# Attention followed by a squared-ReLU feed-forward: the matrix engine takes the two products of the feed-forward in runs of four steps instead of two

## The chip, the cores and the metric

The kernel runs on one core of a Trainium2 chip. The metric is the device time of one execution in microseconds (us); the median of several executions is compared. The engines of a core work side by side, each through its own instructions in order: PE (TensorE, matrix products), ACT (ScalarE), DVE (VectorE), POOL (GpSimd) and SP (SyncE, which here only issues DMAs). In the profile PE is split into the matmuls (PE) and the loads of their stationary operand (PEld).

## The reference

```python
# attention: 4 batches, 8 heads, 768 rows, 64 columns
k_sum = k.reshape(B, H, nb, 32, D).max(axis=3)          # one key per block of 32
v_sum = v.reshape(B, H, nb, 32, D).mean(axis=3)
scores_l = scale * q @ k^T                               # only |i - j| < 16 counts
scores_s = scale * q @ k_sum^T + log(32)
a = softmax(concatenate([scores_l masked, scores_s]))
x = a @ concatenate([v, v_sum])                          # 3072 tokens x 512
# feed-forward
h = x @ w_in                                             # 3072 x 2048
g = s * relu(h) ** 2 + b
out = g @ w_out                                          # 3072 x 512
```

## The kernel before, in words

The 3072 tokens are taken in 12 **chunks** `c` of 256 tokens (three to a batch), and the 2048 hidden columns in 16 slices `f` of 128. One (chunk, slice) is a **step** `i = 16 c + f`; there are 192. A step has:

- `hidden(c, f)` on PE (line 364): the first product, `ph`. From the second chunk on each operand is split into a high and a low part (`wh`, `wl`, `xh`, `xl`), so that a slice is 12 matmuls of 256 columns: four `wl_in` with `xh`, four `wh` with `xl`, four `wh` with `xh`.
- `activate(c, f)`: ACT takes the ReLU out of PSUM (line 371) and squares it (372), POOL makes `g = s r + b` (382), DVE rounds it to `gh` (384) and takes the rest `gl` (386).
- `project(c, f)` on PE (line 401): the second product, for each half of the chunk's tokens `gl` with `wh`, `gh` with `wl_out` and `gh` with `wh`: six matmuls of 512 columns a step, summed over all 16 slices in two banks `po`. At the chunk's end `evict` copies `po` out (409) and SP sends it (412).

While the feed-forward of one chunk runs, the attention of the next is done between its steps, in four units `p` of two heads: `scores` into `ps` (PE, 266), `masked` (DVE, 285), `exps` (ACT, 298), `normalize` (DVE, 305 to 308), `transposes` of the probabilities into `pt` (PE, 314), `turned`, their copy `pT` (ACT, 321), `values` into `pav` (PE, 334, which reads `pT` and the windows `vw`), and `attended`, which copies `pav` to `xh` and `xl` (347, 349). POOL's `fill_k` and `fill_v` (239, 244) put the block keys and values beside the windows.

The order is written out by hand. `at(step, order, fn, ...)` puts a call into a table, and the table is played by step and, within a step, by these classes:

```python
LOAD, SPLIT, ATT, WEIGHTS, HID, PE_ATT, CHAIN, PROJ, EVICT = range(9)
```

Each engine gets its instructions in that order. An attention unit stands at `base` (two steps before the middle or the end of the chunk ahead of its own; units come in twos) plus a lag for each of its parts, from the lists `lags`. Two lines set the order of the products:

```python
at(i if c == 0 else i - i % 2, HID, hidden, c, f)
at(i + LAG if i + LAG < NF else (i + LAG) | 1, PROJ, project, c, f)
```

So from the second chunk on PE does the first product of two steps, then the second product of the two steps before them, and so on. The results of the first product lie in `ph` tiles of one step each; there are two of them, each in a PSUM bank of its own (banks 2 and 3). `gh` and `gl` have four buffers each. All eight banks are in use.

Of the kernel before, what the change touches and what calls it, by code (L numbers as in the profile page):

```python
# [10 lines left out]
F32 = mybir.dt.float32  # L11
F32R = mybir.dt.float32r
# [6 lines left out]
P = 128  # L19
# [7 lines left out]
KR = WIN + NB  # L27
NSUB = 4
T = NSUB * SUB
# [5 lines left out]
NF = DFF // P  # L35
NEG = -8.0e9
LAG = 2


def win_start(st):  # L40
    return min(max(SUB * st - WINDOW, 0), S - WIN)
# [3 lines left out]
def windowed_attention_then_relu2_ffn(ctx, tc, qk, vwin, kt, vt, kq, vrow, wp, sb, out):  # L45


    nc = tc.nc
# [5 lines left out]
    p2 = ctx.enter_context(tc.tile_pool(name="p2", bufs=2))  # L54
    p3 = ctx.enter_context(tc.tile_pool(name="p3", bufs=3))
    ps_po = ctx.enter_context(tc.tile_pool(name="ps_po", bufs=2, space=bass.MemoryType.PSUM))
    ps_h = ctx.enter_context(tc.tile_pool(name="ps_h", bufs=2, space=bass.MemoryType.PSUM))
# [31 lines left out]
    def at(step, order, fn, *args):  # L89
        plan[step].append((order, len(plan[step]), fn, args))  # L90
# [5 lines left out]
    for base, sign in ((0, 1), (BLOCK - 1, -1)):  # L96
        nc.gpsimd.affine_select(
            out=mean4[:, KR - 4 : KR], in_=mean4[:, KR - 4 : KR], compare_op=ALU.is_ge, fill=0.0,
            base=base, pattern=[[-sign * BLOCK, 4]], channel_multiplier=sign,
# [112 lines left out]
    def place(c):  # L212
        return c // PER_B, c % PER_B

    qk_t, vw_t, ps_of, pr_of, mn_of, sm_of, pt_of, pT_of, o_of, xt = ({} for _ in range(10))
# [33 lines left out]
    def scores(c, p, j):  # L249
        q, kw = qk_t[c, p]  # L250
        if j == 0:
            if c == 0 and p % 2:
                both = [ps_h.tile([P, T], F32, name="ps", tag="ph") for _ in range(2)]
                ps_of[c, p] = [t[:, : 2 * KR].rearrange("p (j k) -> p j k", k=KR) for t in both]
            elif c < 2:
                ps_of[c, p] = [ps_s.tile([P, 4, KR], F32, name="ps", tag="ps") for _ in range(2)]
            elif p % 2 == 0:
                both = [ps_s.tile([P, 4, KR], F32, name="ps", tag="ps") for _ in range(2)]
                ps_of[c, p], ps_of[c, p + 1] = [t[:, :2] for t in both], [t[:, 2:] for t in both]
        for e in range(2):  # L260
            r = slice(64 * e, 64 * e + 64)
            for a in range(2):
                i = 2 * j + a
                o, qi = ps_of[c, p][e][64 * a : 64 * a + 64, j], q[r, i * SUB : (i + 1) * SUB]
                if c > 0:
                    nc.tensor.matmul(o, qi, kw[r, i, :], start=True, stop=True)  # L266
                    continue
                w = win_start(i)
                nc.tensor.matmul(o[:, :WIN], qi, kraw[0, p][r, w : w + WIN], start=True, stop=True)
                nc.tensor.matmul(o[:, WIN:], qi, ksum[0, p][r], start=True, stop=True)  # L270
# [78 lines left out]
            nc.vector.tensor_tensor(xt[c][1][:, kcs], o, xt[c][0][:, kcs].bitcast(F32), ALU.subtract)  # L349


    ph_of, gg, po = {}, {}, {}

    def hidden(c, f):
        ph = ph_of[c, f] = ps_h.tile([P, T], F32, name="ph", tag="ph")
        if c == 0:
            terms = [(w_f["in", f], xt[c][0], kc) for kc in range(NKC)]
        else:
            xh, xl = xt[c]
            terms = [  # L360
                (w["in", f], x, kc) for w, x in ((w_l, xh), (w_h, xl), (w_h, xh)) for kc in range(NKC)
            ]
        for n, (w, x, kc) in enumerate(terms):
            nc.tensor.matmul(  # L364
                ph, w[:, kc * P : (kc + 1) * P], x[:, kc], start=(n == 0), stop=(n == len(terms) - 1)
            )

    def activate(c, f):
        ph = ph_of.pop((c, f))
        r = p2.tile([P, T], F32, name="r")  # L370
        nc.scalar.activation(r, ph, AF.Relu)  # L371
        nc.scalar.activation(r, r, AF.Square)  # L372
        if c == 0:
            g = p2.tile([P, T], F32, name="g0", tag="gh", bufs=4)
            if f < 2:
                nc.vector.tensor_scalar(g, r, s_col, b_col, ALU.mult, ALU.add)
            else:
                nc.scalar.activation(g, r, AF.Identity, bias=b_col, scale=s_col)  # L378
            gg[c, f] = (g,)
            return  # L380
        g = p2.tile([P, T], F32, name="g")
        nc.gpsimd.tensor_scalar(g, r, s_col, b_col, ALU.mult, ALU.add)  # L382
        gh = p2.tile([P, T], F32R, name="gh", tag="gh", bufs=4)
        nc.vector.tensor_copy(gh, g)  # L384
        gl = p2.tile([P, T], F32R, name="gl", bufs=4)
        nc.vector.tensor_tensor(gl, g, gh.bitcast(F32), ALU.subtract)  # L386
        gg[c, f] = gh, gl

# [23 lines left out]
            nc.sync.dma_start(out[r0 : r0 + P, :], o)  # L412


    LOAD, SPLIT, ATT, WEIGHTS, HID, PE_ATT, CHAIN, PROJ, EVICT = range(9)


    FIRST, FIRST_SCALED, FIRST_TURNED = -100, 8, 2
# [9 lines left out]
    }  # L428
    stages = {"K": k_max, "N": normalize, "F": fill_v, "T": transposes, "C": turned, "V": values, "X": attended}
    halves = {"S": scores, "M": masked, "E": exps}  # L430
    for n, name in enumerate(FIRST_ORDER.split()):
        kind, i = name[0], int(name[1:])
# [17 lines left out]
    for c in range(1, NC):  # L450
        bi, ci = place(c)
        for p in range(NPAIR):
            if c == 1:

                base, v_at = (0, 3, 6, 8)[p], 0
                lags = (1, 2, 2, 3, 4, 4, 5, 6, 7)
            else:

                base, v_at = NF * (c - 1) - 2 + 8 * (p // 2), 3 * (p % 2)
                lags = ((1, 2, 2, 3, 6, 4, 5, 8, 9), (2, 3, 4, 5, 6, 6, 7, 8, 9))[p % 2]  # L460
            m, e0, e1, n, fv, tr, tu, va, xa = (base + lag for lag in lags)
            if ci == 0:
                at(base - 7, LOAD, load_k, bi, p)
                at(base - 2, ATT, k_max, bi, p)
                if p < 2:
                    for third in range(3):
                        at(base + v_at - 5 + third, LOAD, load_v, bi, p, third)
                        at(base + v_at - 1 + third // 2, ATT, v_sum, bi, p, third)
                    at(base + v_at + 1, ATT, v_mean, bi, p)
            if (c, p) not in ((1, 0),):  # L470
                at(base - 6, LOAD, load_unit, c, p)
            at(base + v_at, LOAD, load_values, c, p)
            if (c, p) != (1, 0):
                at(base - (1 if c > 1 else 2), ATT, fill_k, c, p)
            for j in range(2):
                at(base, PE_ATT, scores, c, p, j)
                at(m, ATT, masked, c, p, j)
                at((e0, e1)[j], ATT, exps, c, p, j)
            at(n, ATT, normalize, c, p)
            at(fv, ATT, fill_v, c, p)  # L480
            at(tr, PE_ATT, transposes, c, p)
            at(tu, ATT, turned, c, p)
            at(va, PE_ATT, values, c, p)
            if c < 2 or p % 2 == 0:
                at(xa, ATT, attended, c, p)
# [10 lines left out]
    for i in range(NC * NF):  # L496
        c, f = divmod(i, NF)

        at(i if c == 0 else i - i % 2, HID, hidden, c, f)
        at(i, CHAIN, activate, c, f)  # L500
        at(i + LAG if i + LAG < NF else (i + LAG) | 1, PROJ, project, c, f)
        if f == NF - 1:
            at((i + LAG) | 1, EVICT, evict, c)

    with tc.manual_schedule():
        for step in sorted(plan):
# [56 lines left out]
```

## Time and profile before

| | |
|---|---|
| median of 3 runs | 648.74 us (648.46 to 649.2) |
| the profiled execution | 648.77 us |
| its span, first to last instruction | 647.1 us |
| outside the span | 1.67 us |
| PE busy | 630.3 us (97%) |
| DVE, ACT, POOL busy | 332.7, 338.4, 153.8 us |
| mean granted clock of PE | 0.997 |

A busy time is the time that an engine's instructions cover; that of PE is modelled, since its matmuls overlap, and its parts are better read from start to start. Rows below give times from the span's start.

### The profile page before, as it was taken

Reading aid. Unit: us, or ns where it says so; the run is one execution under the profiler, and the core shown is the slowest. Engines: PE = TensorE matmul, PEld = TensorE weight load, DVE = VectorE, ACT = ScalarE, POOL = GpSimd, SP = SyncE. Lnnn points to the kernel's source line nnn. Section 1 sums busy time; section 2 is a strip of 40 time slices with the busy share of each in tenths; the row PEclk is TensorE's granted clock in tenths of the full one; section 3 lists DMA queues with packets and bytes.
Section 4 is the critical chain, followed back from the end, with each engine's and each line's share of the span. In section 5 each row is a group of like instructions: output and inputs, shape, how many; then the busy total and the mean of one; then the engine's idle time right before and its main releaser. Section 6 shows DMA issues by size and latency. Waiting matters only on the chain.

```text
span 647.1 us, 13906 instructions
## 1 busy us (share of the span) xinstructions
PE 630.3 (97%) x5164; PEld 549.1 (85%) x5164; DVE 332.7 (51%) x1088; ACT 338.4 (52%) x986; POOL 153.8 (24%) x324
## 2 busy tenths in 40 slices
PE   6799999999999999999999999999999999999997
PEld 4566568989989899898999899898998989999996
DVE  5799988885443434356434434447443353342221
ACT  4899998845444435535435345444444444452322
POOL 3000004143133132232231331331322322312221
PEclk9999999999999999999999999999999999999999
DMA  9999405035203204124402301504420320100000
GB/s 323 386 383 355 131 1 187 1 102 191 72 1 104 72 2 139 49 84 141 141 1 63 115 2 34 153 23 132 146 66 2 105 72 2 57 3 1 33 2 33
DMA packets 25604, 63.25 MB, mean 98 GB/s; under 512 B 3968, under 2 KB 3968, under 8 KB 25536
## 3 DMA queue, kind: packets, MB, share of 16 engines
q1 hardware_dynamic: 25536, 62.36, 29.3%
q8 instruction: 41, 0.67, 0.4%
q14 instruction: 27, 0.22, 0.1%
HBM read 55.90 MB, written 6.29 MB: 96 GB/s over the span
## 4 chain that ended last, share of the span: by engine, by line
PE 86%; ACT 7%; DMA 4%; DVE 2%; issue 0%; SPq 0%; DVEq 0%
PE po L401 39%; PE ph L364 38%; PE pav L334 4%; PE ps L266 3%; PE pt L314 3%; DMA wraw<-in_wp_dram 3%; ACT wraw L116 2%; ACT wraw L117 2%; ACT g L378 1%; DMA kq<-in_kq_dram 1%; ACT pr L298 1%; ACT r L372 1%; ACT r L371 0%; DVE wf_out L134 0%; DVE wf_out L132 0%; DVE wf_in L132 0%
## 5 line engine op out<-in xcount | busy, mean ns | idle before, releaser
L382 POOL TENSOR_SCALAR g<-r,sb_col 128x256 f32<-128x256 f32 x176 | 101.7, 578 | 418.5 <-ACT r L372 322.0
L384 DVE CAST gh<-g 128x256 fp32r<-128x256 f32 x176 | 52.4, 298 | 269.9 <-POOL g L382 269.6
L371 ACT ACTIVATE r<-ph 128x256 f32<-128x256 f32 x192 | 73.4, 382 | 203.8 <-PE ph L364 203.2
L401 PE MATMUL po<-wh,gl 128*128 128x512 f32 x352 | 143.2, 407 | 0.0
L401 PE MATMUL po<-wh,gh 128*128 128x512 f32 x352 | 138.6, 394 | 0.0
L401 PE MATMUL po<-wl_out,gh 128*128 128x512 f32 x352 | 137.7, 391 | 0.0
L364 PE MATMUL ph<-xh,wl_in 128*128 128x256 f32 x704 | 110.9, 280 | 0.0
L364 PE MATMUL ph<-xl,wh 128*128 128x256 f32 x704 | 108.7, 276 | 0.0
L364 PE MATMUL ph<-xh,wh 128*128 128x256 f32 x704 | 108.7, 276 | 0.0
L364 PEld LDWEIGHTS ph<-xh,wl_in 128*128 128x128 f32 x704 | 100.2, 188 | 8.2 <-ACT r L372 0.5
L364 PEld LDWEIGHTS ph<-xl,wh 128*128 128x128 f32 x704 | 93.8, 188 | 0.0
L364 PEld LDWEIGHTS ph<-xh,wh 128*128 128x128 f32 x704 | 92.9, 188 | 0.0
L372 ACT ACTIVATE r<-r 128x256 f32<-128x256 f32 x192 | 80.4, 419 | 6.1
L386 DVE TENSOR_TENSOR gl<-g,gh 128x256 fp32r<-128x256 f32 x176 | 76.4, 434 | 6.0
L401 PEld LDWEIGHTS po<-wh,gh 128*128 128x128 f32 x352 | 66.1, 188 | 14.3
L401 PEld LDWEIGHTS po<-wh,gl 128*128 128x128 f32 x352 | 66.2, 188 | 14.1 <-issue 3.0
L401 PEld LDWEIGHTS po<-wl_out,gh 128*128 128x128 f32 x352 | 66.3, 188 | 11.5
L298 ACT ACTIVATE pr<-pr,mn 128x120 f32<-128x120 f32 x176 | 67.4, 386 | 3.5 <-DVE mn L285 3.3
L321 ACT COPY pT<-pt 120x512 f32<-120x512 f32 x48 | 28.2, 587 | 37.0 <-PE pt L314 36.8
L364 PEld LDWEIGHTS ph<-x,wf_in 128*128 128x128 f32 x128 | 25.0, 200 | 14.3 <-issue 2.6
L244 POOL COPY vw<-vsum 24x256 f32<-24x256 f32 x80 | 36.8, 500 | 1.3
L308 DVE TENSOR_TENSOR pr<-pr,rs 128x480 f32<-128x480 f32 x48 | 35.4, 737 | 1.7
(71 smaller groups left out, 615.6 us busy)
## 6 DMA issues: line engine op xcount, KB each, us to landing
wraw<-in_wp_dram SPq DMA_DIRECT2D x32, 512.0 KB, 10.0
qk<-in_qk_dram SPq DMA_DIRECT2D x44, 368.0 KB, 4.7
vw<-in_vwin_dram SPq DMA_DIRECT2D x48, 192.0 KB, 4.2
out_dram<-o SPq DMA_DIRECT2D x24, 256.0 KB, 2.0
kraw<-in_kt_dram SPq DMA_DIRECT2D x12, 384.0 KB, 3.4
vraw<-in_vt_dram SPq DMA_DIRECT2D x12, 252.0 KB, 4.7
kq<-in_kq_dram SPq DMA_DIRECT2D x4, 512.0 KB, 4.6
vraw<-in_vt_dram SPq DMA_DIRECT2D x6, 264.0 KB, 7.0
```

What stands on the lines that cost most here:

```text
L244: filler(c).tensor_copy(vw_t[c, p][WIN:KR, e], vsum[bi][WIN : WIN + NB, 2 * p + e, :].unsqueeze(1).to_broadcast([NB, NSUB, D]),)
L298: nc.scalar.activation(pr, pr, AF.Exp, bias=mn_of[c, p][:, n : n + 1], scale=-1.0, accum_out=sm_of[c, p][:, n : n + 1])
L308: nc.vector.tensor_tensor(pr, pr, rs.unsqueeze(2).to_broadcast([P, 4, KR]), ALU.mult)
L321: nc.scalar.copy(pT_of[c, p], pt_of.pop((c, p))[:KR])
L334: nc.tensor.matmul(o[64 * e : 64 * e + 64, i * SUB : (i + 1) * SUB], vw[:, e, i, :], pT[:, e * T + i * SUB : e * T + (i + 1) * SUB], start ...
L364: nc.tensor.matmul(ph, w[:, kc * P : (kc + 1) * P], x[:, kc], start=(n == 0), stop=(n == len(terms) - 1))
L371: nc.scalar.activation(r, ph, AF.Relu)
L372: nc.scalar.activation(r, r, AF.Square)
L382: nc.gpsimd.tensor_scalar(g, r, s_col, b_col, ALU.mult, ALU.add)
L384: nc.vector.tensor_copy(gh, g)
L386: nc.vector.tensor_tensor(gl, g, gh.bitcast(F32), ALU.subtract)
L401: nc.tensor.matmul(po[t], a[:, t * P : (t + 1) * P], w, start=(f == 0 and n == 0), stop=(f == NF - 1 and n == len(terms) - 1),)
```

## The change

Steps before 48 keep their order on PE. From the fourth chunk on (`n = 4`) the first products of four steps stand together, and then the second products of the four steps before them. For that `ph` becomes a tile of two steps, one whole bank, so that two such tiles hold four steps; the third chunk, still in twos, uses one tile for each two. `gh` and `gl` get eight buffers, and a scratch area for DMA descriptors is made smaller. From unit (4, 2) on, the lags of the attention units change, `fill_k` stands a step earlier, the transposes of the second unit of each two move ahead of the first products (the new class `TURN`), and the copy of the first unit's transposes moves to the class `CHAIN` of its step.

```diff
     def hidden(c, f):
-        ph = ph_of[c, f] = ps_h.tile([P, T], F32, name="ph", tag="ph")
+        if c < 2 or f % 2 == 0:
+            ph_both[0] = ps_h.tile([P, 2, T], F32, name="ph", tag="ph")
+        ph = ph_of[c, f] = ph_both[0][:, f % 2]
...
-        gh = p2.tile([P, T], F32R, name="gh", tag="gh", bufs=4)
+        gh = p2.tile([P, T], F32R, name="gh", tag="gh", bufs=8)
...
-        gl = p2.tile([P, T], F32R, name="gl", bufs=4)
+        gl = p2.tile([P, T], F32R, name="gl", bufs=8)
...
-    LOAD, SPLIT, ATT, WEIGHTS, HID, PE_ATT, CHAIN, PROJ, EVICT = range(9)
+    LOAD, SPLIT, ATT, WEIGHTS, TURN, HID, PE_ATT, CHAIN, PROJ, EVICT = range(10)
...
                 base, v_at = NF * (c - 1) - 2 + 8 * (p // 2), 3 * (p % 2)
                 lags = ((1, 2, 2, 3, 6, 4, 5, 8, 9), (2, 3, 4, 5, 6, 6, 7, 8, 9))[p % 2]
+                if (c, p) > (4, 1):
+                    lags = ((1, 1, 2, 2, 6, 5, 6, 8, 9), (2, 2, 3, 3, 6, 6, 7, 8, 9))[p % 2]
...
-                at(base - (1 if c > 1 else 2), ATT, fill_k, c, p)
+                at(base - (2 if c == 1 or (c, p) > (4, 1) else 1), ATT, fill_k, c, p)
...
-            at(tr, PE_ATT, transposes, c, p)
-            at(tu, ATT, turned, c, p)
+            at(tr, PE_ATT if not (c, p) > (4, 1) or p % 2 == 0 else TURN, transposes, c, p)
+            at(*((tu, ATT) if not (c, p) > (4, 1) or p % 2 else (tr, CHAIN)), turned, c, p)
...
-        at(i if c == 0 else i - i % 2, HID, hidden, c, f)
+        n = (1, 2, 2, 4)[min(c, 3)]
+        done = i + LAG if i + LAG < NF else (i + LAG) | 1 if n < 4 else (i + 4) | 3
+        at(i - i % n, HID, hidden, c, f)
         at(i, CHAIN, activate, c, f)
-        at(i + LAG if i + LAG < NF else (i + LAG) | 1, PROJ, project, c, f)
+        at(done, PROJ, project, c, f)
         if f == NF - 1:
-            at((i + LAG) | 1, EVICT, evict, c)
+            at(done, EVICT, evict, c)
...
-    nc = _bacc.Bacc("TRN2", target_bir_lowering=False, num_devices=1)
+    nc = _bacc.Bacc("TRN2", target_bir_lowering=False, num_devices=1, dynamic_dma_scratch_size=2048)
```

PE's order around the transposes of a second unit (`pt`), in a middle chunk. Before, they stand between a first product (`ph`, its last two rows shown) and a second (`po`):

```order
L364 MATMUL ph<-xl,wh_1093 128x256 x4
L364 MATMUL ph<-xh,wh_1093 128x256 x4
L314 MATMUL pt<-ident,pr 120x128 x4
L401 MATMUL po<-wh_980,gl 128x512
L401 MATMUL po<-wl_out_985,gh 128x512
```

Now, in a middle chunk too, they stand between the end of a run of `po` and a run of `ph`, of which the first half is shown:

```order
L403 MATMUL po<-wl_out_1270,gh 128x512
L403 MATMUL po<-wh_1265,gh 128x512
L314 MATMUL pt<-ident,pr 120x128 x4
L366 MATMUL ph<-xh,wl_in_1533 128x256 x4
L366 MATMUL ph<-xl,wh_1531 128x256 x4
L366 MATMUL ph<-xh,wh_1531 128x256 x4
L366 MATMUL ph<-xh,wl_in_1569 128x256 x4
L366 MATMUL ph<-xl,wh_1567 128x256 x4
L366 MATMUL ph<-xh,wh_1567 128x256 x4
```

The transposes moved from behind a run of first products to ahead of one, and that run goes on for 48 matmuls (24 before). In the whole program the unbroken runs of `ph` fall from 103 to 67 and those of `po` from 102 to 66; 16 runs of `ph` now follow a `pt`, and none did before.

The first group of fours, in the fourth chunk: here unit (4, 1) still has the old lags. PE's rows now, from the last slice of the second run of four to the next second product:

```order
L366 MATMUL ph<-xh,wl_in_1267 128x256 x4
L366 MATMUL ph<-xl,wh_1265 128x256 x4
L366 MATMUL ph<-xh,wh_1265 128x256 x4
L314 MATMUL pt<-ident,pr 120x128 x4
L334 MATMUL pav<-pT,vw 64x64 x16
L266 MATMUL ps<-qk 64x120 x16
```

Before, a run of `po` and one of `ph` stood between `pt` and `pav`; here, and here alone among the chunks in fours, nothing does.

ACT's order in one group of fours, from the third step of a run on (`r<-ph` is the ReLU, `r<-r` the square, `[waits ...]` the engines it waits for by semaphore, and numbers are tiles: `ph_7121` holds two steps):

```order
L373 ACTIVATE r_7172<-ph_7121 128x256 [waits PE_49,Pool_49]
L374 ACTIVATE r_7172<-r_7172 128x256 [waits Activation_49]
L321 COPY pT_7186<-pt_7181 120x512 [waits PE_49]
L373 ACTIVATE r_7188<-ph_7121 128x256 [waits Pool_49]
L374 ACTIVATE r_7188<-r_7188 128x256 [waits Activation_49]
L411 COPY o_7221<-po_6736 128x512 [waits DMAHW6_49,PE_49]
L411 COPY o_7224<-po_6737 128x512 [waits DMAHW7_49,PE_49]
L373 ACTIVATE r_7288<-ph_7238 128x256 [waits PE_49,Pool_49]
L374 ACTIVATE r_7288<-r_7288 128x256 [waits Activation_49]
L321 COPY pT_7297<-pt_7233 120x512
L373 ACTIVATE r_7299<-ph_7238 128x256 [waits Pool_49]
```

The second ReLU of a tile has no wait on PE of its own: the first has waited for both steps of the tile. The second unit's copy `pT_7297` now stands behind the first ReLU and square of the next run of four.

## Rows read from the trace of the kernel before

**Rows 1.** The page: busy us (share of the span) x instructions

```profile
PE 630.3 (97%) x5164; PEld 549.1 (85%) x5164; DVE 332.7 (51%) x1088; ACT 338.4 (52%) x986; POOL 153.8 (24%) x324
```

**Rows 2.** The page: the chain that ended last, shares by engine

```profile
PE 86%; ACT 7%; DMA 4%; DVE 2%; issue 0%; SPq 0%; DVEq 0%
```

**Rows 3.** Busy by stretch: PE, PEld, DVE, ACT, POOL, clock, DMA share, GB/s

```profile
50.00:100.00 50.00, 48.12 (x293) 31.67 (x294) 45.04 (x121) 48.45 (x121) 1.87 (x4) 1.00 0.47 146
150.00:205.00 55.00, 55.00 (x469) 49.96 (x468) 24.34 (x89) 26.61 (x84) 14.22 (x29) 1.00 0.27 86
400.00:500.00 100.00, 100.00 (x863) 90.66 (x862) 47.92 (x165) 45.67 (x145) 26.98 (x56) 1.00 0.29 90
```

**Rows 4.** The chain in order of time: start, us, engine, tile, line, count

```profile
217.49 2.95 PE po L401 x12
...
242.64 2.95 PE po L401 x12
...
604.93 2.75 PE po L401 x12
...
637.88 5.51 PE po L401 x24
```

**Rows 5.** PE in time order, last chunk: start us, us of the group, line

```profile
602.02 0.64 PE L364 MATMUL ph<-xh,wl_in 128*128 128x256 f32 x4
...
603.40 0.62 PE L364 MATMUL ph<-xh,wl_in 128*128 128x256 f32 x4
...
604.76 0.39 PE L401 MATMUL po<-wh,gl 128*128 128x512 f32 x1
```

**Rows 6.** All engines in time order, the run of `po` that ends the span

```profile
637.72 0.39 PE L401 MATMUL po<-wh,gl 128*128 128x512 f32 x1
...
642.99 0.40 PE L401 MATMUL po<-wh,gh 128*128 128x512 f32 x1
```

**Rows 7.** All engines in time order, a pair of steps with transposes

```profile
401.80 0.64 PE L364 MATMUL ph<-xh,wl_in 128*128 128x256 f32 x4
...
403.45 0.39 ACT L371 ACTIVATE r<-ph 128x256 f32<-128x256 f32 x1
...
403.87 0.42 ACT L372 ACTIVATE r<-r 128x256 f32<-128x256 f32 x1
...
404.55 0.60 PE L314 MATMUL pt<-ident,pr 128*120 128x128 f32 x4
404.91 0.48 PE L401 MATMUL po<-wh,gl 128*128 128x512 f32 x1
...
405.19 0.59 ACT L321 COPY pT<-pt 120x512 f32<-120x512 f32 x1 [0.91 <-PE pt L314]
...
405.36 0.43 DVE L386 TENSOR_TENSOR gl<-g,gh 128x256 fp32r<-128x256 f32 x1
...
407.76 0.63 PE L364 MATMUL ph<-xh,wl_in 128*128 128x256 f32 x4
```

**Rows 8.** The transposes as a group: count, busy us, mean ns of one

```profile
L314 PE MATMUL pt<-ident,pr 128*120 128x128 f32 x128 | 19.2, 272 | 0.0
```

**Rows 9.** All engines in time order: first product, `values`, `scores`, second product

```profile
415.99 0.62 PE L364 MATMUL ph<-xh,wh 128*128 128x256 f32 x4
...
416.53 1.15 PE L334 MATMUL pav<-pT,vw 120*64 120x64 f32 x32
...
417.62 1.05 PE L266 MATMUL ps<-qk 64*64 64x120 f32 x32
...
418.60 0.50 PE L401 MATMUL po<-wh,gl 128*128 128x512 f32 x1
...
418.94 0.39 PE L401 MATMUL po<-wl_out,gh 128*128 128x512 f32 x1
...
419.17 0.39 PE L401 MATMUL po<-wh,gh 128*128 128x512 f32 x1
```

More of the change, by code (lines that the diff above doesn't have):

```diff
@@ L252, in scores @@
             if c == 0 and p % 2:
-                both = [ps_h.tile([P, T], F32, name="ps", tag="ph") for _ in range(2)]
-                ps_of[c, p] = [t[:, : 2 * KR].rearrange("p (j k) -> p j k", k=KR) for t in both]
+                both = [ps_h.tile([P, 2, T], F32, name="ps", tag="ph") for _ in range(2)]
+                ps_of[c, p] = [t[:, 0, : 2 * KR].rearrange("p (j k) -> p j k", k=KR) for t in both]
             elif c < 2:
@@ L349, in attended @@
             nc.vector.tensor_tensor(xt[c][1][:, kcs], o, xt[c][0][:, kcs].bitcast(F32), ALU.subtract)
-    ph_of, gg, po = {}, {}, {}
+    ph_of, ph_both, gg, po = {}, {}, {}, {}
     def hidden(c, f):
-        ph = ph_of[c, f] = ps_h.tile([P, T], F32, name="ph", tag="ph")
+        if c < 2 or f % 2 == 0:
+            ph_both[0] = ps_h.tile([P, 2, T], F32, name="ph", tag="ph")
+        ph = ph_of[c, f] = ph_both[0][:, f % 2]
         if c == 0:
@@ L373, in activate @@
         if c == 0:
-            g = p2.tile([P, T], F32, name="g0", tag="gh", bufs=4)
+            g = p2.tile([P, T], F32, name="g0", tag="gh", bufs=8)
             if f < 2:
```

## The prediction, made before the changed kernel ran

> **What bounds the kernel now.** I began with the page's busy times: PE covers 97% of the span, and no other engine much over half [rows 1]. The shares of the chain that ended last say the same from the other side: 86% of it is PE, and what is not PE lies in the loading at the start and the sending at the end [rows 2]. Then I looked at busy time by stretch, to see where PE is not covered. It is short of work only ahead of 100 us (48.12 of 50 us); from 150 us on, PE covers every stretch whole [rows 3]. The fourth chunk, where the change begins on PE, starts near 195 us, so the part that is changed has no idle time of PE left to remove. What is left to win there is inside the covered time: matmuls that follow each other more slowly than they could. For that one reads starts, not durations.
>
> The chain in order of time gives the rhythm. In the last chunk, which has no attention beside it, six pairs of steps take from 604.93 to 637.88 us: 32.95 / 6 = 5.492 us a pair [rows 4]. In the chunks with attention eight steps take from 217.49 to 242.64, 25.15 us [rows 4]. The difference from four bare pairs (21.97 us) is two units' transposes, values and scores.
>
> **The change part by part.** *Fewer passages between the two products.* How much of a pair's 5.492 us belongs to the passage? The run of `po` that ends the span has 24 matmuls; from its first start to its last there are 23 spacings in 642.99 - 637.72 = 5.27 us [rows 6], 0.2291 each, so 12 in the middle of a run take 2.749. In the run of `ph`, the first step takes 603.40 - 602.02 = 1.38 us and the second 604.76 - 603.40 = 1.36 [rows 5]; other pairs print the same two values within 0.01. So 24 matmuls in the middle of a run take 2.72. The pair would take 2.749 + 2.72 = 5.469 without a passage, and takes 5.492: a passage costs 0.023 us, and it lies in the first matmuls of `ph`. The order shows 36 runs of `ph` fewer (103 to 67): 36 x 0.023 = 0.83 us less. The starts are printed to 0.01 us, so the price may be 0.01 to 0.04, and the term 0.4 to 1.4 us.
>
> The Trainium skill, in "TensorE: Matmul & The Clock Gate", section "Back-to-back issue gap", gives the spacing of matmuls as their columns by the clock plus a fixed 2.5 ns, with nothing for a change from one product to another. By that rule this change has nothing to remove, and the first term of the sum would be 0. The trace does not quite agree: 0.2291 us for 512 columns is more than its 0.216, and the first and the second step of one run differ though their columns are the same.
>
> *The transposes in a new place.* 16 groups of transposes move from between `ph` and `po` to between `po` and `ph`. In the old place, a pair with transposes takes 407.76 - 401.80 = 5.96 us from `ph` to `ph` (5.95 in the neighbouring pair), 0.46 more than a bare one [rows 4, 7]. Four transposes at their own spacing, (0.60 - 0.272) / 3 = 0.109 us each [rows 7, 8], are 0.44; so 0.02 is paid at the two edges. The new place is not in the trace. From below: nothing is paid at the edges and the run of `ph` behind them begins at full pace, 0.02 + 0.02 saved, 0.7 us over 16. From above: the edges cost what those of values and scores cost. `ph` to `pav` takes 416.53 - 415.99 = 0.54 us for four matmuls that take 0.45 within a run, and the first spacing of `po` behind `ps` is 0.34 against 0.23 [rows 9]: 0.09 + 0.11 = 0.20 a group, 0.18 more than now, 2.9 us over 16. I take no change, since the transposes use the whole array as the feed-forward does (128 by 120), and their edges today cost a tenth of those of the 64-wide matmuls; that is the row that they are nearest to.
>
> *One new wait.* In the first groups of fours the transposes of unit (4, 1) stand right ahead of the values. PE issues them in 404.91 - 404.55 = 0.36 us; the copy `pT` begins 0.64 us after their start and takes 0.59, so it is there 1.23 us after it [rows 7]. PE has the values of unit (4, 0) to do first, half of 417.62 - 416.53 = 1.09, so 0.55 us [rows 9], with 0.09 for the edge. It comes to the second unit at 0.36 + 0.09 + 0.55 = 1.00 and waits 0.23, with the hand-over some 0.3 us. Behind it wait the scores and a run of `po`, so all of it is paid, once. Bounds 0 and 0.6. ACT's three ReLUs behind that copy come late by as much, and have a run of `po` of 5.5 us ahead of their tile's next use.
>
> *Whole-bank tiles and the later ReLU.* The first ReLU of a tile now waits for both steps, 1.36 us later than before. The Trainium skill ("PSUM — Partial Sum Buffer", section "PSUM bank collisions raise a hardware error") asks that a read of a bank be guarded against PE's writes by the bank, not by the address, and the waits in the new order are of that kind. No run here shows a collision. It costs nothing as long as the chain behind the ReLU has time: from a ReLU's start to the end of its `gl` it is 405.79 - 403.45 = 2.34 us [rows 7]. For the last two steps of a four, in line on ACT behind each other with a `pT` between (0.81 + 0.59 + 0.81, then POOL and DVE about 1.5), it is about 4 us. Until `project` needs it, PE has a run of `po` (5.5) and one of `ph` (5.46): 11 us. The tile itself is written again after one run of `po`, 5.5 us at the earliest. In the third chunk, in twos, the same delay stands against a slack of about 4 to 5 us (`gl` at 405.79, its `po` behind the next run of `ph` that starts at 407.76). So nothing is paid. At the end of the program the last four steps have a run of `po` of 5.5 us as cover, and nothing is paid either.
>
> *The second unit's copy.* `pT` of the second unit is behind the first ReLU and square of the next four, which wait for two steps: 0.36 + 2.74 + 0.3 + 0.81 + 0.59 = 4.8 us after the transposes' start. PE wants it after four steps and the first unit's values: 0.36 + 5.46 + 0.09 + 0.55 = 6.46. Slack 1.7 us: nothing is paid, but this is the thinnest cover.
>
> *Nothing is paid* for the rest: the lags put masking, exponentials and normalizing a step earlier or as before, with eleven microseconds from the scores to the first transposes; `fill_k` a step earlier on POOL, busy a quarter of the span; the eviction two steps later, with a run of `ph`, the values and the scores (7.5 us) ahead of the next use of `po` and two copies of 0.6 us to do; on SP the output follows later, and loads ahead of it no longer wait for it. The buffers of `gh` and `gl` are not waited for by PE, and the smaller scratch serves no DMA that the page shows.
>
> **Sum.** 648.77 - 0.83 + 0 + 0.3 = 648.24 us, made against the profiled execution, which is 0.03 above the median. I predict **648.2**, 0.1% under the median of before. A measurement of this kernel can tell about 0.2%, 1.3 us, from no change: the forecast is no change, with a small minus.
>
> **The rivals.**
> *The passage is no saving (0.12).* The first matmuls of `ph` may be slow in proportion to the run of `po` ahead of them, so that half as many passages cost twice as much. Against it: a run of `po` is 2.75 us and the slowness 0.023; for it, only that the trace has one length of run. Time 648.77 + 0.3 = 649.1, the same side. It is also the time by the skill's rule above.
>
> *All the edges are worth more (0.16).* The passage is worth 0.04 and the moved transposes lose both their edges: 648.77 - 1.4 - 0.7 + 0.3 = 647.0, 0.27% under the median. For it: everything on PE is back to back, so each nanosecond counts. Against: it needs the upper end of both.
>
> *Slower: the transposes' new edges (0.14).* Between `po` and `ph` they cost what values and scores do: 648.24 + 2.9 = 651.1, 0.37% over. It decides from 0.11 us a group on (1.8 us over 16). For it: PE has never done this passage in the trace, and it changes the stationary operand's kind twice. Against: `pt` to `po` is such a change too, and costs 0.02.
>
> *Slower: the second unit's copy is late (0.04).* If ACT is 1.7 us later than I reckon, PE stands at each of 16 values; at 0.15 us each that is 2.4 us, 650.6.
>
> **Chances.** The forecast itself has 0.54, within 647.5 to 649.0. With the first rival, within 0.2% holds 0.66; faster is 0.16 and slower 0.18, the other rivals. For eight in ten the range reaches into both outer cases, 647.0 to 650.3.
>
> **What would show it.** In the trace after, the eight-step period falls from 25.15 us to about 25.10; within a run of 48 only the first step takes 1.38 us and the other three 1.36; `pt` between `po` and `ph` adds 0.46 to its pair. Near 210 us (the values of that step stand at about 215 before, behind two runs of `po` more) stands one wait of PE on `pT` of about 0.3 us, and no wait of PE besides in the changed part. What would make it wrong: repeated idle time of PE ahead of `pav` (the copy is late) or `ph` (a ReLU is late), or a first spacing of `ph` behind `pt` well over 0.12 us.

## The result, and the profile after

The changed kernel takes 650.47 us (median of 11 runs, 649.42 to 651.64), before 648.89 beside it on the same chip (11 runs). The ratio is 1.003, 95% interval 1.0022 to 1.0038: slower by 0.3%, where 648.2 and no change were forecast. The profiled execution took 650.34 us, 1.57 more than that of before. In the profiled execution of before, and not in that of the changed kernel, the granted clock falls to 0.50 near 31 us, ahead of the changed part; executions with a mean granted clock of 0.997 or less, as it then is, take some 0.3 to 1.4 us longer than others of the same kernel.

Busy time cannot show where the loss lies. On the page of the changed kernel PE is covered as before [rows 1]; its 0.4 us more are less than the 1.57.

```profile
PE 630.7 (97%) x5164; PEld 549.1 (85%) x5164; DVE 332.6 (51%) x1088; ACT 334.2 (52%) x986; POOL 162.1 (25%) x324
```

The chain in order of time shows it (start, us, engine, tile, line, count), with one group of eight steps whole:

```profile
164.64 1.08 PE pav L334 x32
...
386.61 1.08 PE pav L334 x32
394.38 5.47 PE ph L366 x48
406.23 5.66 PE ph L366 x48
411.88 1.08 PE pav L334 x32
419.65 5.47 PE ph L366 x48
...
538.25 1.08 PE pav L334 x32
```

From `pav` to `pav` six groups take 538.25 - 386.61 = 151.64 us, 25.27 each. The forecast was 25.10, and before it was 25.15 [rows 4]. Each group has two runs of 48 `ph`, with the same operands but for the slices. The first, between `po` and the first unit's transposes, takes 5.47 us. The second, between the second unit's transposes and `pav`, takes 5.66. There are 15 such runs, and 15 x 0.19 = 2.9 us. Why is the second slow? PE alone in time order, groups of four matmuls, both runs:

```profile
405.63 0.60 PE L314 MATMUL pt<-ident,pr 128*120 128x128 f32 x4
405.99 0.72 PE L366 MATMUL ph<-xh,wl_in 128*128 128x256 f32 x4
406.54 0.63 PE L366 MATMUL ph<-xl,wh 128*128 128x256 f32 x4
...
411.25 0.64 PE L366 MATMUL ph<-xh,wh 128*128 128x256 f32 x4
411.81 1.15 PE L334 MATMUL pav<-pT,vw 120*64 120x64 f32 x32
...
419.49 0.64 PE L366 MATMUL ph<-xh,wl_in 128*128 128x256 f32 x4
419.96 0.62 PE L366 MATMUL ph<-xl,wh 128*128 128x256 f32 x4
...
424.50 0.62 PE L366 MATMUL ph<-xh,wh 128*128 128x256 f32 x4
424.96 0.60 PE L314 MATMUL pt<-ident,pr 128*120 128x128 f32 x4
```

In each run the starts of the second and of the twelfth group of four are 40 matmuls apart: 4.71 us in the one (117.7 ns a matmul), 4.54 in the other (113.5). The loss is not at an edge and not a wait. It is a slower pace that lasts from the first matmul of the run to its last. The quick run begins at it too: its first four matmuls take 419.96 - 419.49 = 0.47 us, and by the single starts its first five spacings are 117 to 123 ns and the rest 112 to 115. Busy by stretch for those two pieces (the columns as in [rows 3]):

```profile
406.54:411.25 4.71, 4.71 (x42) 4.71 (x41) 0.54 (x2) 1.98 (x5) 0.56 (x1) 1.00 0.97 316
419.96:424.50 4.54, 4.54 (x42) 4.54 (x41) 0.46 (x4) 2.31 (x10) 0.55 (x1) 1.00 0.00 0
```

The granted clock is 1.00 in both (2.4 GHz). Beside the slow one ACT does less, POOL as much, and DVE 0.08 us more in a stretch that is 0.17 longer. Transfers run beside the slow one and not beside the quick one; this looks like a cause, and the experiments show that it is none. Below, a run of `ph` is called quick at 113 ns a matmul and slow at 118.

The kernel before has both paces too. PE in time order in its second chunk, a quick run of 24 and the next, a slow one, both at a granted clock of 1.00:

```profile
94.72 0.62 PE L364 MATMUL ph<-xh,wh 128*128 128x256 f32 x4
95.17 0.62 PE L364 MATMUL ph<-xh,wl_in 128*128 128x256 f32 x4
...
100.91 0.64 PE L364 MATMUL ph<-xh,wh 128*128 128x256 f32 x4
101.38 0.63 PE L364 MATMUL ph<-xh,wl_in 128*128 128x256 f32 x4
```

Four matmuls take 0.45 us in the one and 0.47 in the other. This is its only slow run. In the changed kernel 16 runs of 48 stand right behind transposes, and one of them is quick: the first, at 203.21 us.

The other terms came as forecast. The first group in fours, all engines in time order:

```profile
208.78 0.60 PE L314 MATMUL pt<-ident,pr 128*120 128x128 f32 x4
...
209.31 1.48 PE L334 MATMUL pav<-pT,vw 120*64 120x64 f32 x32
...
209.41 0.58 ACT L321 COPY pT<-pt 120x512 f32<-120x512 f32 x1 [2.28 <-PE pt L314]
```

`pav` prints 1.48 us for 1.15 [rows 9], a wait of 0.33 us for the copy `pT`. And the runs of four steps in the last chunk, PE in time order:

```profile
606.38 0.64 PE L366 MATMUL ph<-xh,wl_in 128*128 128x256 f32 x4
...
607.77 0.62 PE L366 MATMUL ph<-xh,wl_in 128*128 128x256 f32 x4
...
609.13 0.62 PE L366 MATMUL ph<-xh,wl_in 128*128 128x256 f32 x4
...
610.49 0.62 PE L366 MATMUL ph<-xh,wl_in 128*128 128x256 f32 x4
...
617.34 0.64 PE L366 MATMUL ph<-xh,wl_in 128*128 128x256 f32 x4
```

Only the first step takes 1.39 us, the others 1.36, and four steps take 617.34 - 606.38 = 10.96, two pairs before 10.98 [rows 4]: one passage less, 0.02 us.

### The profile page after: what moved, and what is told of

The parts are those of the page before. It is cut to its first block, busy times and chain, and to the rows that moved or that the text cites. A ratio compares the mean times of both kernels' runs of the same rounds, so it can differ in the third digit from the quotient of the medians.

```text
span 648.6 us, 13856 instructions
## 1 busy us (share of the span) xinstructions
PE 630.7 (97%) x5164; PEld 549.1 (85%) x5164; DVE 332.6 (51%) x1088; ACT 334.2 (52%) x986; POOL 162.1 (25%) x324
## 4 chain that ended last, share of the span: by engine, by line
PE 86%; ACT 9%; DMA 3%; issue 0%; SPq 0%; DVE 0%
PE po L403 39%; PE ph L366 38%; PE pav L334 4%; PE ps L266 3%; PE pt L314 3%; ACT wraw L116 3%; ACT wraw L117 3%; DMA wraw<-in_wp_dram 3%; ACT pr L298 1%; ACT g L380 1%; ACT r L374 1%; DMA kq<-in_kq_dram 1%; ACT r L373 1%; ACT pT L321 0%; ACT wh L143 0%
## 5 line engine op out<-in xcount | busy, mean ns | idle before, releaser
L384 POOL TENSOR_SCALAR g<-r,sb_col 128x256 f32<-128x256 f32 x176 | 109.4, 621 | 403.7 <-ACT r L374 346.1
L366 PE MATMUL ph<-xh,wl_in 128*128 128x256 f32 x704 | 112.5, 282 | 0.0
L366 PEld LDWEIGHTS ph<-xh,wl_in 128*128 128x128 f32 x704 | 96.7, 188 | 3.8 <-ACT r L374 0.5
L388 DVE TENSOR_TENSOR gl<-g,gh 128x256 fp32r<-128x256 f32 x176 | 78.9, 449 | 6.0
L366 PE MATMUL ph<-x,wf_in 128*128 128x256 f32 x128 | 30.9, 384 | 5.1 <-DVE wf_in L134 2.9
```

The lines of the kernel that those rows point to most:

```text
L366: nc.tensor.matmul(ph, w[:, kc * P : (kc + 1) * P], x[:, kc], start=(n == 0), stop=(n == len(terms) - 1))
```

## The experiments

Edits are against the changed kernel, and `...` marks lines left out; `f % 8 == 4` marks the first slice of a run in question. Counted from the starts of the matmuls, the changed kernel has 31 stretches of 24 `ph` at the slow pace out of 88 (two in each of the 15 runs, and one in the second chunk), and the kernel before has 1 (slow: the median spacing is over 115.5 ns). The table gives this count for each kernel; where there is no ratio, one execution was timed.

| kernel | us | ratio to before (95%) | slow of 88 |
|---|---|---|---|
| wait_at_first | 650.74 | 1.0032 (1.0019 to 1.0044) | 31 |
| wait_at_thirteenth | 650.79 | 1.0033 (1.0022 to 1.0045) | 31 |
| transposes_inside_po | 650.67 | 1.0033 (1.0021 to 1.0046) | 31 |
| twos_with_whole_bank_tiles | 649.41 | 1.0013 (1.0004 to 1.0022) | 1 |
| act_wait | 651.01 | 1.0032 (1.0019 to 1.0045) | 31 |
| act_covered | 651.30 | 1.0033 (1.0021 to 1.0046) | 31 |
| early_unit_4_0 | 654.17 | 1.0075 (1.0061 to 1.0089) | 33 |
| no_odd | 641.13 | | 1 |
| no_even | 644.46 | | 31 |
| odd_inside_ph | 648.31 | 0.9998 (0.9989 to 1.0007) | 1 |
| even_inside_ph | 650.70 | 1.0040 (1.0026 to 1.0053) | 38 |
| extra_odd_transpose | 653.67 | 1.0081 (1.0068 to 1.0095) | 45 |
| extra_even_transpose | 652.80 | | 45 |
| extra_short_ph | 649.58 | 1.0012 (1.0003 to 1.0021) | 1 |
| odd_inside_all | 650.08 | 1.0019 (1.0010 to 1.0028) | 2 |
| extra_odd_one_later | 652.64 | | 45 |
| no_even_one_later | 644.67 | | 31 |

**Does a wait set the pace?** The 15 runs of `ph` in question begin without a wait of their own (the transposes ahead carry it); most of the others wait on ACT at their first matmul. In two kernels POOL rewrites one column of the first or the second slice's weights two steps ahead, so that the run waits on POOL at its first or its thirteenth matmul:

```
+    def touch(f):
+        w = w_l["in", f][:, 0:1]
+        nc.gpsimd.tensor_copy(w, w.bitcast(F32))
...
+        if c > 2 and c < NC - 1 and f % 8 == 4 and (c, f) != (3, 4):
+            at(i - 2, ATT, touch, f + 0)     # the second kernel: f + 1
```

> The changed kernel, but GpSimd rewrites one column of wl_in of slices 4 and 12 with its own value two steps ahead, so that the first matmul of each of the 15 runs of ph behind transposes carries a semaphore wait of its own (long fulfilled). Theory W (a run of ph that begins without a wait of its own stays at 118 ns a matmul, one that begins with a wait falls to 113 after five): the 15 runs fall from 5.83 to about 5.63 us, the eight-step period from 25.27 to 25.07, and the time by 15 x 0.2 = 3.0 us to about 0.997 of the kernel before. Theory T (transposes right ahead of ph make the run slow): the runs stay at 118 ns, the time at about 1.003 of before. Theory P (GpSimd's fills beside these runs slow PE): as T.

> The same rewriting, of wl_in of slices 5 and 13: the wait stands at the 13th matmul of the 15 runs instead of the first. If any wait lets the run fall to the quick pace (W, wide): 118 ns for 17 matmuls, then 113, so 31 x 4.7 ns = 0.15 us a run and 2.2 us in all are won, 0.9995 of before. If only a wait at the run's start does (W, narrow; the changed kernel has a wait at the 25th matmul of these runs and they stay slow): no change, 1.003. T and P: no change, 1.003.

Both stay slow: the times and the 31 slow stretches are those of the changed kernel. Then with ACT's semaphore (`nc.scalar.copy`, one step ahead), and the counterpart, where the wait of runs at 113 ns is carried by the `po` ahead of them:

```
+        if c > 2 and c < NC - 1 and f % 8 == 4 and (c, f) != (3, 4):
+            at(i - 1, CHAIN, touch, "in", f)                # act_wait
...
+        if c > 2 and f == 8 or c == NC - 1 and f in (4, 12):
+            at(i - 2, CHAIN, touch, "out", (f - 5) % NF)    # act_covered
```

> ScalarE rewrites one column of a weight tile with its own value one step earlier, so that the first matmul of each of the 15 slow runs of 48 ph (those between transposes and pav) waits on ScalarE's own semaphore, as the first matmul of every quick run in the trace does. Theory W2 (a run goes at 113 ns a matmul only when its first matmul carries a wait on ScalarE's semaphore): the 15 runs fall from 5.83 to about 5.6 us, about -3.0 us, 647.5 us, ratio 0.997 to 0.998. Rival D (the state is left by what PE did before, by the second unit's transposes and by that of no wait of the run itself): runs stay at 118 ns a matmul, 5.83 us, and the time stays at 650.6, ratio 1.003.

> The counterpart: ScalarE rewrites one column of the second weights two steps earlier, so that the last twelve po ahead of some runs that are quick now (po, ph 48, with f of 8 in the chunks from the fourth on and three of the last chunk, 11 runs) carry the wait on ScalarE, and the first ph carries none. Theory W2: these 11 runs turn slow, 118 ns a matmul, 43 x 4.5 ns = about 0.2 us each, +2.2 us, 652.7, ratio 1.006. Rival D: they stay at 5.47 us, time stays at 650.6, ratio 1.003.

Those at 118 ns stay there with the wait, and those at 113 ns without it. A wait does not set the pace; this theory fell from both sides.

**Tiles, and transposes right ahead.** One kernel keeps the tiles of two banks and goes back to twos; in another the second unit's transposes stand in the middle of the run of `po`.

```
-        n = (1, 2, 2, 4)[min(c, 3)]
+        n = (1, 2, 2, 2)[min(c, 3)]                         # twos_with_whole_bank_tiles, old lags
...
+            at(*((tr, PE_ATT) if not (c, p) > (4, 1) or p % 2 == 0 else (tr - 1, TURN)), transposes, c, p)
+        at(done, PROJ if n < 4 or f % 4 < 2 else PROJ2, project, c, f)   # TURN now between the two PROJ
```

> The changed kernel's tiles of two steps, eight buffers of gh and gl and small scratch, but in twos to the end with the lags and places of the kernel before. All three theories: the time of before, 1.000 within 0.001, since no run of ph lacks its wait, none follows transposes, and the later ReLU is covered. If the tiles themselves cost time (a rival to all three), 1.002 to 1.003.

> The changed kernel, but the transposes of the second unit stand in the middle of the run of po (after two of its four steps) instead of between po and ph. The run of ph behind it follows po and still begins without a wait of its own. W: these runs stay at 118 ns, 1.002 to 1.004 of before. T: they fall to 113 ns from the sixth matmul on, 15 x 0.2 = 3.0 us less than the changed kernel, about 0.998 of before. P: as W.

With the tiles in twos every run of `ph` in the changed part is quick, and a kernel below has them in fours with every run quick (`odd_inside_ph`), so they do not set the pace. They are not free, though: near the program's end PE's weight load waits for a `gl`, which the later ReLU delays (all engines in time order):

```profile
640.80 0.19 PEld L403 LDWEIGHTS po<-wh,gl 128*128 128x128 f32 x1 [0.42 <-DVE gl L388]
```

The 0.42 us are idle time of the weight load, and PE loses less by it: the last 24 `po` take 643.43 - 637.91 = 5.52 us from the first start to the last, 5.27 before [rows 6], so the tiles cost 0.25 us there. That is all they cost in the traces from the first `ph` of the fourth chunk to the last `po`: 643.43 - 195.32 = 448.11 us, before 642.99 - 195.14 = 447.85. The rest of the 0.9 us in the table lies outside this stretch, and its cause is open. With the transposes 12 matmuls of `po` away the runs stay slow: transposes right ahead are not what it takes.

**The one wait.** The first unit's transposes of the first group in fours move to where later groups have them:

```
-                if (c, p) > (4, 1):
+                if c > 3:   # and tr = 3, tu = 5 for (4, 0); (4, 1) in TURN; copy of (4, 0) at (tr | 3, CHAIN)
```

> The first group in fours moves the first unit's transposes of the fifth chunk to where they stand in all later groups, so that pav no longer waits for their late copy. If the term of one new wait is right (the trace of the changed kernel shows pav ahead of that wait at 1.407 against 1.082 us), the stretch near 210 us gives back 0.3 to 0.45 us; one more run behind transposes may then go at 118 ns a matmul (+0.2). Expected 650.2 to 650.4, ratio 1.0025. Rival (the wait is hidden elsewhere or moves to another tile): no change, 650.6.

A miss. The wait moved and grew, and the granted clock fell in the run of `ph` behind it (time order, then busy by stretch):

```profile
205.94 0.66 PE L314 MATMUL pt<-ident,pr 128*120 128x128 f32 x4 [1.88 <-ACT pT L321]
```

```profile
205.50:208.00 2.50, 2.06 (x15) 2.06 (x16) 1.31 (x4) 1.09 (x3) 1.71 (x4) 0.83 0.91 276
208.00:211.00 3.00, 3.00 (x17) 3.00 (x17) 0.21 (x1) 0.00 (x0) 1.63 (x5) 0.57 0.72 247
```

The second unit's transposes wait 1.88 us for the copy of the first, because there is one tile `pt` and ACT copies the last chunk's output first. After that idle time the granted clock falls to 0.83 and 0.57 of full speed in these stretches, so towards its level of 1.2 GHz, and that run of 48 takes 7.36 us from its first start to that of `pav`. It is at the slow pace as well: back at a clock of 1.00, its fours start at 211.26, 211.73 and 212.21 us, 0.47 to 0.48 apart, so that only about 7.36 - 5.83 = 1.5 us are the clock's. In the changed part this is the one difference between kernels that the clock explains.

**Taking transposes away, or moving them into `ph`.** Two kernels leave out the transposes of one unit of each two, and two move them:

```
+        if (c, p) > (4, 1) and p % 2 == 1:                  # no_odd; no_even: == 0
+            return
...
-        at(i - i % n, HID, hidden, c, f)
+        at(i - i % n, HID if n < 4 or f % 4 < 2 else HID2, hidden, c, f)
+            # odd_inside_ph: the second unit's transposes in TURN_IN, between HID and HID2
+            # even_inside_ph: the first unit's, at tr - tr % 4 in TURN_IN
```

> Left out: the second unit's transposes (15 groups of four, from the sixth chunk's pattern on); ScalarE copies the first unit's result in their place, so the second unit's values are wrong. The slow runs then read po, ph 48, pav. Theory T2 (a run goes slow when two groups of transposes have passed since the last ph): these runs turn quick, about 5.55 us (5.47 and 0.09 more for the passage to pav), and the time falls by 15 x (0.355 + 0.03 + 0.28) = about 10 us, near 640. Rival P (place: what stands behind the run, pav, or the weights' slices of it, makes it slow): 5.75 us, 118 ns a matmul.

> Left out: the first unit's transposes (15 groups of four); the copy takes the result of the unit before. The runs in question read po, pt, ph 48, pav. Theory T2 (two groups since the last ph): quick, about 5.63 us. Rival T1 (transposes directly ahead, or the second unit's, are enough): 5.83 us. Rival P (place): 5.83 us. With the other ablation: quick in both speaks for T2, slow only here for T1, slow in both for P.

> Same computation; the second unit's transposes stand in the middle of the run of 48, behind its second step, as ph 24, pt, ph 24, pav. ScalarE copies them where it did. T2: one group since the last ph, so both halves go at 113 ns: 15 x 0.2 us back, about -2.8 us against the changed kernel, 647.8, ratio 0.998 to 0.9995 of before. T1: first half quick, second half slow: -1.5 us, 649.0. P: both slow, 650.6.

> Same computation; the first unit's transposes move ahead, into the middle of the run of 48 before the first half of po (ph 24, pt, ph 24, po 24, pt, ph 48, pav). T2: one group since the last ph everywhere, all quick: about -2.8 us, 647.8, ratio 0.998 to 0.9995. T1 or P: the run ahead of pav stays at 5.83 us, and the time at 650.6 or a little more.

Without the second unit's transposes all runs of the changed part are quick, though `pav` still stands behind them: the place is no cause. Without the first unit's, something appeared that no theory had. The chain in order of time:

```profile
218.34 5.47 PE ph L372 x48
229.73 5.65 PE ph L372 x48
...
243.16 5.66 PE ph L372 x48
254.76 5.46 PE ph L372 x48
...
267.98 5.47 PE ph L372 x48
279.38 5.65 PE ph L372 x48
```

Runs with transposes ahead (229.73, 254.76, ...) are slow and quick in turn, and so are runs with none ahead (218.34, 243.16, ...). So the rule "two groups of transposes since the last `ph`" fell, and so did "transposes directly ahead". Two of these pieces in busy by stretch also settle the transfers, a slow one with none beside it and a quick one with 0.94:

```profile
243.47:248.18 4.71, 4.71 (x43) 4.71 (x41) 0.54 (x4) 2.39 (x10) 0.56 (x1) 1.00 0.00 0
255.07:259.61 4.54, 4.54 (x43) 4.54 (x42) 0.45 (x2) 1.95 (x5) 0.56 (x1) 1.00 0.94 310
```

With the second unit's transposes in the middle of the run all the runs of the changed part are quick, and the time is that of before, 0.9998 of it (0.9989 to 1.0007). The chain shows the period that was predicted, (536.94 - 386.34) / 6 = 25.10 us:

```profile
386.34 1.08 PE pav L334 x32
...
405.52 2.74 PE ph L366 x24
408.70 2.74 PE ph L366 x24
411.44 1.08 PE pav L334 x32
...
536.94 1.08 PE pav L334 x32
```

The part that was changed is even shorter than before in this trace: from the first `ph` of the fourth chunk to the last `po` it takes 642.88 - 195.58 = 447.30 us, before 447.85, changed 644.52 - 194.64 = 449.88. The 0.55 us do not show in the ratio: 9 of the 11 executions of this kernel, and 6 of the 15 of before beside them, had the mean granted clock of 0.997 or less.

The first unit's transposes in the run before it left the second run slow, and every second time the first half of that run before it too (38 of 88).

**Is the pace carried along PE's stream?** If a run's pace depends on how the stream reaches it, a little more work ahead can turn it, near or far. One kernel doubles a transpose of the second unit, one of the first unit (one run of `po` further away), and one repeats the first product of the run on 32 columns:

```
+        if (c, p) > (4, 1) and p % 2 == 1:                  # extra_even_transpose: == 0
+            nc.tensor.transpose(pt_of[c, p][:KR, 3 * P :], pr[:, 3, :], ident)
...
+            nc.tensor.matmul(ph[:, :32], w[:, kc * P : (kc + 1) * P], x[:, kc, :32], start=True, stop=True)
```

> Same result; the last transpose of the second unit is done twice (five instead of four ahead of the slow runs), which adds 15 x 0.108 = 1.6 us of work. Theory C (the pace of a run is carried over from the phase in which PE's stream reaches it, and any small shift of the stream can turn it): some or all of the 15 runs fall from 5.83 to 5.63 us; if all do, the time falls by 1.4 us to about 649.2 although work was added. Rival T (transposes between po and ph are slow by themselves): runs stay at 5.83, time rises by 1.6 us to about 652.2.

> Same result; the last transpose of the first unit is done twice, one po run of 24 and one group of transposes ahead of the slow runs; 1.6 us of work are added. Theory C: if the phase is carried through po and the transposes, the runs far behind can change pace (some at 5.63 us). Rival T: they stay at 5.83 us, 652.2.

> Same result; the first product of each of the 15 slow runs is preceded by the same product on 32 of its 256 columns (overwritten by the whole one), so that a short matmul stands between the transposes and the run; adds about 15 x 0.06 = 0.9 us. Theory C: the runs can turn quick, then 15 x (0.06 - 0.2) = about -2 us, 648.5. Rival T: they stay slow, 651.5.

The short matmul turned all 15 runs quick. PE in time order:

```profile
405.58 0.60 PE L314 MATMUL pt<-ident,pr 128*120 128x128 f32 x4
405.93 0.26 PE L367 MATMUL ph<-xh,wl_in 128*128 128x32 f32 x1
406.04 0.72 PE L369 MATMUL ph<-xh,wl_in 128*128 128x256 f32 x4
406.60 0.62 PE L369 MATMUL ph<-xl,wh 128*128 128x256 f32 x4
...
411.13 0.62 PE L369 MATMUL ph<-xh,wh 128*128 128x256 f32 x4
411.68 1.15 PE L334 MATMUL pav<-pT,vw 120*64 120x64 f32 x32
```

411.13 - 406.60 = 4.53 for 40, and from the first `ph` to `pav` 5.75 us for 49 matmuls, where the changed kernel takes 411.81 - 405.99 = 5.82 for 48. Work was added, and the ratio fell from 1.0030 to 1.0012. The doubled transposes went the other way: the 15 runs stayed slow, and every second one of the quick runs, which have no transposes ahead of them for two runs, turned slow too (45 of 88).

A chunk is two groups of eight steps, so "every second" could still be something of the chunk's half: its slices, the output, the loads. Two more kernels begin one group later (`(c, p) > (4, 3)`):

> The fifth transpose of the second unit begins one group of eight steps later (14 groups instead of 15). In the earlier run the runs of ph ahead of the first unit's transposes went slow in turn: quick from slice 8 on, slow from slice 0 on, in every chunk. Since a chunk is two such groups, that alternation could belong to the half of the chunk. Theory C (the pace is carried from run to run): begun one group later, the alternation is shifted by one group: slow from slice 8 on and quick from slice 0 on. Rival H (something of the chunk's half: its slices, the eviction, the loads): slow from slice 0 on as before. Time 652 to 653.5 in both.

> The first unit's transposes are left out one group later than before (14 instead of 15 groups, the copy takes the result of the unit before). Theory C: the order of quick and slow runs is shifted by one group: the run ahead of pav quick at slices 12 to 15 and slow at 4 to 7, that of slices 0 to 3 quick and of 8 to 11 slow. Rival H: as before, quick at 4 to 7 and 8 to 11, slow at 12 to 15 and 0 to 3. Time about 644.8 in both.

The chain of the first of these:

```profile
242.21 5.47 PE ph L368 x48
...
267.60 5.66 PE ph L368 x48
...
293.17 5.47 PE ph L368 x48
```

Begun at the earlier group, the same slices have 5.66 near 243, 5.47 near 268 and 5.65 near 294 us; now it is 5.47, 5.66 and 5.47. The kernel without the first unit's transposes shifts in the same way (its runs near 230, 255 and 280 us: 5.66, 5.65, 5.46, before 5.65, 5.46, 5.65). They took 652.64 and 644.67 us. So the pace does not belong to the slices, the loads or the half of the chunk. It depends on what PE's stream went through ahead, over several runs of other work. The order alone does not always settle it: in the second chunk all these kernels have the same order on PE, and of its first two runs of 24, each with one spacing of about 0.52 us at its start, one is slow in every trace, in some the first and in others the second.

**A version beyond.** The transposes in the middle of the run, now in the first group too (against odd_inside_ph):

```
-            at(tr, PE_ATT if not (c, p) > (4, 1) or p % 2 == 0 else TURN_IN, transposes, c, p)
+            at(tr, PE_ATT if c < 4 or p % 2 == 0 else TURN_IN, transposes, c, p)
```

> The version with the second unit's transposes in the middle of the run of ph, now for the first group of fours as well, so that its copy is no longer awaited by pav. If the term of the one wait (0.33 us, pav 1.407 for 1.082) is right: 648.3 falls to about 648.0, ratio 0.9990 to 0.9997 of before, and the trace shows pav at 1.08 near 210 us. Rival (the second transposes now wait for the copy of the first, as when the first unit was moved): as slow as 648.3 or slower.

A miss again; the rival had the right side and the wrong engine. In time order:

```profile
207.68 0.63 PE L314 MATMUL pt<-ident,pr 128*120 128x128 f32 x4 [1.55 <-DVE pr L308]
```

The transposes come before that unit is normalized. The 0.33 us have not been won back; no version here beats the kernel before in the time of whole executions by more than can be measured.

## Why the prediction was wrong, point by point

- *Fewer passages*, 0.83 us: right. Runs of 48 take 5.47 us where they are quick, and with all runs quick the period was the predicted 25.10, and the changed part 0.55 us shorter, where -0.83 + 0.3 = -0.53 were forecast. The rival "the passage is no saving" fell. What I priced as a passage was the beginning of the run at the slow pace: five spacings of 117 to 123 ns for 113 make the 0.02 us.
- *The transposes in a new place*, taken at 0: this step failed. It cost 15 x 0.19 = 2.9 us by the length of the runs, 449.88 - 447.30 = 2.6 by the traces of the changed part; that is near the upper bound, but not by its mechanism. I priced the transposes' edges, and these do cost next to nothing. The first spacing of `ph` behind `pt`, the sign named, is 0.20 us, but this run starts 0.36 us after the first of four transposes that take 0.44, so that it gives back what it had gained; with the same first spacing the kernel with the transposes inside `ph` keeps 25.10. What I took as fixed was the pace of the 48 matmuls behind the edge. The profile of before has the other pace, in the one run of 24 at 99.56 us and at the beginning of every run, and I did not read it as such.
- *One new wait*, 0.3: right, 0.33.
- *Whole-bank tiles, copy, lags, buffers*, 0: no wait of PE appeared with fours, and the thinnest cover, the second unit's copy, held. In twos the later ReLU cost 0.25 us at the end; in fours the last 24 `po` show no such wait, behind the longer run of `po`.
- Sum: with 2.6 for the failed term 648.24 + 2.6 = 650.8. The profiled 650.34 is lower because its unchanged start ran 0.5 us ahead (`pav` at 164.64, before at 165.14); in its trace the granted clock does not fall near 31 us, in that of before it does. The rival "slower: the transposes' new edges" gave 651.1 and the right side for another reason, so its number is luck.

Shown: the pace of the runs is the loss, and it goes with the stream ahead; waits at the run, tiles, transfers, the clock and the place are excluded. Open: where the state is held, and by what rule an order of work leads to one pace or the other. That 15 of 15 runs fell on the slow one here was not to be read from the profile of before.

## What to carry to other kernels

Where PE is covered whole, compare runs of the same matmuls by the spacing of their starts, before and after: busy time and waits stay the same when the pace changes. A price for moving work should allow for the pace of what stands behind it: here 4 ns on each of some 43 matmuls outweighed every edge and wait. When a reorder loses without a wait, try one or two other places for the moved piece before giving it up; putting the same transposes in the middle of the run gave everything back. And read single spacings in the profile of before: a pace that stands there once can come back elsewhere.

## What was not expected of the hardware

The same weight loads and matmuls of 256 columns, back to back at a granted clock of 1.00, go at 113 or at 118 ns each for a whole run, and a matmul of 32 columns ahead can turn one into the other. The Trainium skill, "TensorE: Matmul & The Clock Gate", section "Back-to-back issue gap", gives the columns by the clock and 2.5 ns for the isolated gap of one matmul, so an estimate of 109 ns here; both paces are above it, and a rule with one value cannot tell them apart. The same section of the Trainium skill says that in a stream of weight loads and matmuls, as here, both set the spacing, which the prediction left out; for such a stream it has no value at 256 columns.
